# The end of the last batch: more of the heads by x^T x, and another order behind it

## The chip, the cores and the metric

The kernel runs on one core of a Trainium2 chip. The metric is the device time of one execution in microseconds. Before the change three runs gave 791.0, 791.21 and 795.83 us, median 791.21. Besides, one execution was taken with the hardware profiler; every row of a profile below comes from it.

The engines are named as in the profile: PE is TensorE (matrix products), PEld its loading of weights, DVE is VectorE, ACT is ScalarE, POOL is GpSimd, SP is SyncE, which here only issues DMAs. "SPq" is SP's instruction queue. L303 is line 303 of the kernel before. Each engine works through its own instructions strictly in the order in which the program gives them; semaphores tie the engines together.

## What is computed

Two layers, for 8 batches of 3200 rows of 256 columns. The first is a gated attention without softmax, the second a mixing of tokens:

```python
scores = z @ z.T / S                    # z: 3200 x 64
x = u * (np.maximum(scores, 0) ** 2 @ v)  # x: 3200 x 256

wq = x @ w_q                            # 3200 x 64
wk = x @ w_k                            # 3200 x 64
W_tok = wq @ wk.T / 8
out = np.maximum(W_tok @ x, 0) @ w_out  # 3200 x 256, float32
```

The second layer has no function between its first two products, so the kernel never forms `W_tok`. It builds the small matrix `wk.T @ x` (64 x 256, called the heads) from all rows of a batch, and then `wq @ heads` (the mix). Since `wk = x @ w_k`, the heads are also `w_k.T @ (x.T @ x)`: part of the rows can be brought in by x^T x, a 256 x 256 matrix, without their keys `wk`.

## The kernel before

**Tiling.** A batch of 3200 rows is cut into seven groups, numbered from 0: six of 512 rows and a last one of 128 (`widths`, L39; `LASTG` = 6). A tile is 128 rows. For each group the scores come from PE, pass through ACT or DVE (relu) and ACT or POOL (square), partly through a DMA transpose, since the scores are symmetric, and are multiplied with v on PE into two PSUM banks for each half group (L303). When a half group is finished, `gate` copies the one bank on ACT (L319), adds the other on DVE (L320), and multiplies with u on POOL into `x_sb` (L335).

**The second layer in the loop.** SP transposes x by DMA (`turn_x`, L349), PE forms queries and keys (`projections`, L366), ACT casts them to 16 bits (L379), SP transposes the keys by DMA (`turn_keys`, L384), PE multiplies keys with x into the heads (`heads`, L393). Heads are made in two portions per batch: groups 0 to 2, then the others. PE computes them in two halves of the array's rows; DVE adds them up (L406, L409, L410) into `ha`, and because one sum lies in the wrong half of the partitions, two small DMAs carry each half to the other (`cross_heads`, L415, tile `hx`), after which DVE adds again (L420, in the last batch L423). Then come, per group, the mix on PE (`mix`, L429), a relu on ACT (`mix_out`, L444 and L446, tile `rt`), the product with `w_out` on PE (`proj`, L456), the scaling (`proj_out`, ACT L484 or DVE L479) and the store by SP (L485).

**What sets the order.** The program is written out in order at build time. A small planner (L519 to L911) holds a model clock of each engine; it emits the products with v one after another and fits the other work between them, where its model says that inputs have arrived. Transfers of SP are `move`s: each has a time from which it may go and a time at which it is due, and is sent in order of the due time. `keys_landed` (L636) starts a portion of the heads when the model has all its keys. Whatever is left over when the products with v are all emitted is drained in L899 to L912.

**The last batch.** Behind the loop nothing is left to hide the second layer of the last groups. So groups 5 and 6 of batch 7 have no keys: DVE makes a second copy `xd` of their x (L329) in a free tile of pool `pz`, and `last_gram` (L495, products L499) accumulates x^T x of both in one PSUM bank. Their queries come late, by `projections` with the tile name `qq`. To have something to do meanwhile, the mixes of groups 4 and 5 of the batch before, batch 6, are put aside (`kept`, L670) and done at the end. The tail behind L913 is written out by hand:

1. x^T x of group 5; mix of the first kept group; x^T x of group 6; mix of the second kept group;
2. x^T x copied to SBUF as `G`, one half on DVE (L936), the other on ACT (L937), the second waiting for the first; PE multiplies it with `w_k` in 32 bits (`last_heads`, L509, tile `hl`); DVE adds the other groups' heads and writes `hs` (L941);
3. projection and store of the first kept group, half on ACT, half on DVE;
4. queries of groups 5 and 6 (`qq`);
5. projection and store of the second kept group;
6. mix of group 0, then for each group the mix of the next and its own projection and store.

**Buffers that matter here.** PSUM tiles of `ps_tile` (L75) have two slots, shared by scores, queries, mixes and projections; the tail's `acc_tile` uses the four banks of the products with v. `rt` has two buffers (`prt`, L71): the relu of one group must wait until the projection of the group before the last has read its own. In the tail the stores all go through SP, in order.

Of the kernel before, what the change touches and what calls it, by code (L numbers as in the profile page):

```python
# [16 lines left out]
def kernel(  # L17
# [10 lines left out]
    nc = tc.nc  # L28

    B, S, D = u.shape  # L30
# [12 lines left out]
    assert sum(widths) == S and dqk == 64 and dh == 64 and ND == 2  # L43

    FAR = 2

    GSCALE = 4.0
    C1 = GSCALE * GSCALE
# [29 lines left out]
    def acc_tile(half, r, name, dtype=FP32):  # L78
        n = W if dtype == FP32 else 2 * W
        return pacc.tile([P, n], dtype, tag=f"acc{half}{r}", name=name)  # L80
# [232 lines left out]
    def gate(b, gi, half):  # L313
        if (b, gi) not in xs:
            assert len(xs) < NX, (b, gi, list(xs))
            xs[b, gi] = px.tile([P, 2, NC, 2, dh], FP16, tag="x_sb", name="x_sb")
        n = min(2, widths[gi] // P - 2 * half)
        both = psum.tile([P, 2 * D], FP32, tag="both", name="both")
        nc.scalar.copy(out=both[:, 0 : n * D], in_=accs[half, 0][:, 0 : n * D])  # L319
        nc.vector.tensor_add(  # L320
            out=both[:, 0 : n * D], in0=accs[half, 1][:, 0 : n * D], in1=both[:, 0 : n * D]
        )
        if b == B - 1 and gi >= LASTG - 1:
            if gi < LASTG and half == 0:
                spare = pz.tile([P, NT, 2, dqk], FP16, tag="zd", name="xd")
                spare = spare[:].rearrange("p n a k -> p (n a k)")
                xds[LASTG - 1] = spare[:, 0 : 4 * D].rearrange("p (n d) -> p n d", d=D)
                xds[LASTG] = spare[:, 4 * D : 5 * D].rearrange("p (n d) -> p n d", d=D)
            nc.vector.tensor_mul(  # L329
                out=xds[gi][:, 2 * half : 2 * half + n, :].rearrange("p n d -> p (n d)"),  # L330
                in0=both[:, 0 : n * D],
                in1=us[b, gi][:, 2 * half : 2 * half + n, :].rearrange("p n d -> p (n d)"),
            )
        for r in [half] if widths[gi] == W else range(2):
            nc.gpsimd.tensor_mul(  # L335
                out=xs[b, gi][:, 0:n, :, r, :].rearrange("p n c d -> p (n c) d"),
                in0=both[:, 0 : n * D].rearrange("p (m d) -> p m d", d=dh),
                in1=us[b, gi][:, 2 * half : 2 * half + n, :].rearrange(
                    "p n (c d) -> p (n c) d", d=dh
                ),  # L340
            )
        if 2 * half + n == widths[gi] // P:
            us.pop((b, gi))
# [37 lines left out]
    def turn_keys(b, gi):  # L381
        nn = widths[gi] // P
        ks[b, gi] = pk.tile([P, 4, 2, dh], FP16, tag="kx", name="kx")
        nc.sync.dma_start_transpose(  # L384
            out=ks[b, gi][:, 0:nn, :, :].rearrange("p n a h -> p n (a h)"),
            in_=qks[b, gi][:].rearrange("p r s -> p (r s)")[:, 0 : nn * P],
        )
# [60 lines left out]
    def proj(b, gi, banks):  # L448
        rt = rts.pop((b, gi))
        nj = widths[gi] // P  # L450
        for r in halves(gi):
            n = min(2, nj - 2 * r)
            flat = rt[:, r, :, :].rearrange("p d s -> p (d s)")
            for dc in range(ND):
                for j in range(n):
                    nc.tensor.matmul(  # L456
                        out=banks[r][:, ds(j * D, D)],
                        lhsT=flat[:, ds((dc * n + j) * P, P)],
                        rhs=wo[:, dc, :],
                        start=(dc == 0 and j == 0),  # L460
                        stop=(dc == ND - 1 and j == n - 1),
                    )

    def proj_out(b, gi, banks, ways, stores=None):
        n0 = starts[gi] // P
        if stores is None:
            fo = pg.tile([P, 2, W], FP32, tag="g", name="fo")
        else:
            fo = pg.tile([P, 2, W], FP32, tag="fo", name="fo", bufs=2)
        flat_out = fo[:].rearrange("p a w -> p (a w)")  # L470
        at = 0
        for on_dve, queue, n in ways:
            sl = slice(at * D, (at + n) * D)
            if isinstance(banks, list):
                part = banks[at // 2][:, 0 : n * D]
            else:
                part = banks[:].rearrange("p a w -> p (a w)")[:, sl]
            if on_dve:
                nc.vector.tensor_scalar(  # L479
                    out=flat_out[:, sl], in0=part, scalar1=FINAL_SCALE, scalar2=None,  # L480
                    op0=AOP.mult,
                )
            else:
                nc.scalar.mul(out=flat_out[:, sl], in_=part, mul=FINAL_SCALE)  # L484
            store = lambda queue=queue, at=at, n=n, sl=sl: queue.dma_start(  # L485
                out=rows(out, b)[:, n0 + at : n0 + at + n, :],
                in_=flat_out[:, sl].rearrange("p (n d) -> p n d", d=D),
            )
            if stores is None:
                store()  # L490
            else:
                stores.append(store)
            at += n

    def last_gram(b, gi, ps):  # L495
        nj = widths[gi] // P
        for n in range(nj):
            for cc in range(ND):
                nc.tensor.matmul(  # L499
                    out=ps[:, ds(cc * D, D)],  # L500
                    lhsT=xds[gi][:, n, ds(cc * P, P)],
                    rhs=xds[gi][:, n, :],
                    start=(gi < LASTG and n == 0 and cc == 0),
                    stop=(gi == LASTG and n == nj - 1 and cc == ND - 1),
                )

# [33 lines left out]
    def at_time(t, fn):  # L540
        later.append((t, fn))

    def move(ready, due, issue, takes, fn, landed=None, may=None):
        moves.append((ready, due, issue, takes, fn, landed, may))
# [74 lines left out]
    def use_keys(b, gi):  # L619
        open_slot()  # L620
        ps = ps_tile("qk")
        projections(b, gi, ps)
        clock[PE] += 0.44 if gi < LASTG else 0.24
        ready = clock[PE] + FROM_PE
        projections_out(b, gi, ps)
        done = give(ACT, ready, 0.56)
        n = widths[gi] / P
        move(
            done + SLACK, done + 10.0, 1.28, 0.21 * n, lambda: turn_keys(b, gi),
            lambda t: at_time(t, lambda: keys_landed(b, gi)), lambda: len(ks) < NK,  # L630
        )
        close_slot(done)

    FIRST_HEADS = range(3)

    def keys_landed(b, gi):  # L636
        keyed.append((b, gi))
        for gis in FIRST_HEADS, range(3, NG if b < last else LASTG - 1):
            if gi in gis and all((b, i) in keyed for i in gis):
                add_extra(clock[PE] + 0.5, "heads", lambda gis=gis: use_heads(b, gis))  # L640

# [273 lines left out]
    def mixed(b, gi, i=None):  # L915
        if i is None:
            ps = ps_tile("mx")
            banks = [ps[:, 0, :], ps[:, 1, :]]
        else:
            ps = banks = [acc_tile(h, i % 2, "mx")[:] for h in range(len(halves(gi)))]  # L920
        mix(b, gi, banks)
        mix_out(b, gi, ps)

    def projected(b, gi, ways):
        ps = ps_tile("fo")
        proj(b, gi, [ps[:, 0, :], ps[:, 1, :]])
        proj_out(b, gi, ps, ways)

    both_ways = [(False, nc.sync, 2), (True, nc.sync, 2)]
    psg = acc_tile(1, 0, "xtx")  # L930
    last_gram(last, LASTG - 1, psg)
    mixed(*kept[0])
    last_gram(last, LASTG, psg)
    mixed(*kept[1])
    g32 = pg.tile([P, ND * D], FP32, tag="g", name="G")
    nc.vector.tensor_copy(out=g32[:, 0:D], in_=psg[:, 0:D])  # L936
    nc.scalar.copy(out=g32[:, D : 2 * D], in_=psg[:, D : 2 * D])  # L937
    psl = acc_tile(1, 1, "hl")
    last_heads(last, g32, psl[:, 0:D])
    hss[last] = psml.tile([P, D], FP16, tag="hs", name="hs")  # L940
    nc.vector.tensor_add(out=hss[last][:], in0=psl[:, 0:D], in1=hacc[last][:, 1, :])  # L941
    banks = [acc_tile(0, r, "fo") for r in range(2)]
    proj(*kept[0], banks)
    proj_out(*kept[0], banks, both_ways)
    for gi in (LASTG - 1, LASTG):
        ps = ps_tile("qq")
        projections(last, gi, ps)
        projections_out(last, gi, ps)
    projected(*kept[1], both_ways)
    for gi in range(NG):  # L950
        if gi == 0:
            mixed(last, 0, 0)
        if gi < LASTG:
            mixed(last, gi + 1, gi + 1)
        nj = widths[gi] // P
        projected(last, gi, [(True, nc.sync, nj)] if gi != LASTG - 1 else both_ways)


# [28 lines left out]
```

## Time and profile before

| what | value |
|---|---|
| median of 3 runs | 791.21 us (791.0 to 795.83) |
| profiled execution | 790.96 us, its span 789.2 us |
| PE, products | busy 763.2 us (97%) |
| PE, loading of weights | 645.7 us (82%) |
| DVE / ACT / POOL | 479.4 (61%) / 551.8 (70%) / 612.9 us (78%) |
| last product with v | begins at about 760.7 us |
| PE's longest idle time after that | 5.15 us, before 769.48 |
| stores in the tail | 12, issued between 773.07 and 786.18 us |

The span runs from the first to the last instruction of the profiled execution; the time of an execution is slightly longer. For nearly the whole span PE has work without a pause; the change concerns the last 5% or so. There the shares of busy time over the whole span say nothing; what counts is the timeline of each engine in that stretch, and, for each idle time, what ended it. A row of a timeline gives start, duration, engine, line, operation, output and inputs, and in square brackets the idle time of that engine before the row and its releaser. Rows of the same kind in a series are merged, and x8 at the end is their number.

### The profile page before, as it was taken

To read this page: it belongs to the slowest core of one execution; us is meant where nothing else is said; L and a number is where in the kernel's file an instruction comes from. 1 tells how busy PE (TensorE), PEld (TensorE's weight loads), DVE (VectorE), ACT (ScalarE), POOL (GpSimd) and SP (SyncE) were. 2 spreads that over 40 slices of the span, in tenths; PEclk is the share of its full clock that TensorE was granted. 3 is DMA by queue.
4 is the path that set the end of the run, shared out by engine and by line. 5 is a ranking of instruction groups with operands and counts; after the bars stand their busy time and mean duration, and the time that the engine had idled before them with its cause. 6 is when DMAs were issued, how large, how long until landed. Compare 5 with 4: busy or idle time off the path is not lost.

```text
span 789.2 us, 28159 instructions
## 1 busy us (share of the span) xinstructions
PE 763.2 (97%) x12373; PEld 645.7 (82%) x12373; DVE 479.4 (61%) x479; ACT 551.8 (70%) x659; POOL 612.9 (78%) x418
## 2 busy tenths in 40 slices
PE   6989999999999999999999999999999999999976
PEld 5879898887888888888788887988788888888864
DVE  5755577664685656754587635666468654675634
ACT  5766478766776677786687678866778767777624
POOL 7887799886998769877798876888789775787830
PEclk9999999999999999999999999999999999999998
DMA  7999999999999979999999999999999998899425
GB/s 192 146 172 165 177 160 179 156 225 194 204 184 189 220 164 194 152 189 216 210 162 170 187 214 199 177 151 208 193 207 165 178 225 160 183 163 194 122 56 220
DMA packets 310636, 142.57 MB, mean 181 GB/s; under 512 B 287985, under 2 KB 291953, under 8 KB 310513
## 3 DMA queue, kind: packets, MB, share of 16 engines
q1 hardware_dynamic: 303600, 124.60, 83.4%
q0 software_dynamic: 6768, 15.98, 14.8%
q8 instruction: 96, 1.57, 0.9%
q14 instruction: 28, 0.22, 0.1%
q10 hardware_dynamic: 144, 0.20, 0.1%
HBM read 59.64 MB, written 26.21 MB: 109 GB/s over the span
## 4 chain that ended last, share of the span: by engine, by line
PE 91%; DVE 3%; DMA 2%; issue 1%; ACT 1%; POOL 1%; SPq 0%; DVEq 0%; POOLq 0%; ACTq 0%
PE acc L303 66%; PE sc L224 12%; PE fo L456 6%; PE qk L366 3%; DVE g L247 2%; PE hd L393 1%; PE mx L429 1%; DVE both L320 1%; DMA v_sb<-in_v_dram 1%; DMA hx<-ha 1%; ACT both L319 1%; POOL x_sb L335 1%; DVE ha L410 0%; DMA z<-in_z_dram 0%; SPq L349 0%
## 5 line engine op out<-in xcount | busy, mean ns | idle before, releaser
L262 POOL TENSOR_TENSOR at<-g 128x1024 f16<-128x1024 f32 (+2 forms) x245 | 451.5, 1858 | 82.5 <-DVE g L247 66.5
L303 PE MATMUL acc<-v_sb,at 64*128 64x256 f16 x7312 | 499.1, 270 | 5.0 <-DVE both L320 2.5
L247 DVE TENSOR_SCALAR g<-sc 128x1024 f32<-128x1024 f32 (+2 forms) x309 | 363.9, 1197 | 153.0 <-PE sc L224 137.6
L303 PEld LDWEIGHTS <-at 64*128 64x128 f16 x7312 | 393.0, 94 | 66.8 <-issue 12.7
L260 ACT ACTIVATE at<-g 128x1024 f16<-128x1024 f32 x223 | 229.4, 1036 | 30.7 <-DVE g L247 27.2
L243 ACT ACTIVATE g<-sc 128x1024 f32<-128x1024 f32 (+1 forms) x159 | 159.2, 1003 | 60.5 <-PE sc L224 59.8
L335 POOL TENSOR_TENSOR x_sb<-both,u_sb 128x512 f16<-128x512 f32 (+1 forms) x112 | 134.4, 1207 | 64.4 <-DVE both L320 63.8
L224 PE MATMUL sc<-zT 64*128 64x512 f16 x920 | 180.2, 378 | 3.5 <-DVE g L247 3.1
L303 PE MATMUL acc<-v_sb,tt 64*128 64x256 f16 x2304 | 158.7, 269 | 0.0
L320 DVE TENSOR_TENSOR both<-acc,both 128x512 f32<-128x512 f32 (+1 forms) x104 | 69.1, 670 | 128.9 <-ACT both L319 128.4
L303 PEld LDWEIGHTS <-tt 64*128 64x128 f16 x2304 | 123.3, 94 | 11.6 <-issue 0.4
L319 ACT COPY both<-acc 128x512 f32<-128x512 f32 (+1 forms) x104 | 58.4, 566 | 65.5 <-PE acc L303 63.5
L224 PEld LDWEIGHTS <-zT 64*128 64x128 f16 x920 | 56.8, 94 | 17.6 <-issue 12.4
L484 ACT ACTIVATE fo<-fo 128x1024 f32<-128x1024 f32 (+2 forms) x50 | 44.9, 908 | 23.5 <-PE fo L456 22.1
L446 ACT ACTIVATE rt<-mx 128x1024 f16<-128x1024 f32 (+1 forms) x49 | 45.1, 931 | 22.1 <-PE mx L429 21.8
L456 PE MATMUL fo<-wo,rt 128*128 128x256 f16 x400 | 53.1, 276 | 1.2 <-ACT rt L444 0.6
L456 PEld LDWEIGHTS <-rt 128*128 128x128 f16 x400 | 35.4, 98 | 15.6 <-issue 9.6
L379 ACT CAST qk<-qk 128x512 f16<-128x512 f32 (+1 forms) x54 | 29.4, 544 | 21.6 <-PE qk L366 21.6
L366 PE MATMUL qk<-xT_sb,wqk 64*128 64x256 f16 (+1 forms) x404 | 32.2, 265 | 0.1
L366 PEld LDWEIGHTS <-wqk 64*128 64x128 f16 x416 | 22.8, 94 | 2.5 <-issue 0.5
L303 PE MATMUL acc<-v_sb,ttl 64*128 64x256 f16 x384 | 24.6, 269 | 0.0
L303 PEld LDWEIGHTS <-ttl 64*128 64x128 f16 x384 | 19.7, 94 | 3.5 <-issue 0.8
(42 smaller groups left out, 163.9 us busy)
## 6 DMA issues: line engine op xcount, KB each, us to landing
u_sb<-in_u_dram SPq DMA_DIRECT2D x48, 512.0 KB, 5.1
out_dram<-fo SPq DMA_DIRECT2D x45, 512.0 KB, 4.7
v_sb<-in_v_dram POOLq DMA_DIRECT2D x35, 320.0 KB, 6.0
zn<-in_z_dram POOLq DMA_DIRECT2D x7, 400.0 KB, 5.7
tt<-at SPq DMA_TRANSPOSE x144, 4.4
out_dram<-fo SPq DMA_DIRECT2D x6, 256.0 KB, 2.1
u_sb<-in_u_dram SPq DMA_DIRECT2D x8, 128.0 KB, 3.9
hx<-ha SPq DMA_DIRECT2D x16, 64.0 KB, 4.7
```

The costliest lines, as they stand in the source:

```text
L224: nc.tensor.matmul(out=sc[:, h, 0:gw], lhsT=zT[b][top(h), ts(ti, P)], rhs=zT[b][top(h), ds(gs, gw)], start=True, stop=True,)
L243: nc.scalar.activation(out=g[:, hs, 0:w], in_=sc[:, hs, 0:w], func=RELU, scale=GSCALE)
L247: nc.vector.tensor_scalar(out=g[:, hs, 0:w], in0=sc[:, hs, 0:w], scalar1=0.0, scalar2=GSCALE, op0=AOP.max, op1=AOP.mult,)
L260: nc.scalar.square(out=out, in_=g[:, hs, 0:w])
L262: nc.gpsimd.tensor_mul(out=out, in0=g[:, hs, 0:w], in1=g[:, hs, 0:w])
L303: nc.tensor.matmul(out=accs[half, r][:, ds((j % 2) * D, D)], lhsT=weights(b, gi, ti, j)[top(r), :], rhs=vs[b][top(r), ti, :], start=(first ...
L319: nc.scalar.copy(out=both[:, 0 : n * D], in_=accs[half, 0][:, 0 : n * D])
L320: nc.vector.tensor_add(out=both[:, 0 : n * D], in0=accs[half, 1][:, 0 : n * D], in1=both[:, 0 : n * D])
L335: nc.gpsimd.tensor_mul(out=xs[b, gi][:, 0:n, :, r, :].rearrange("p n c d -> p (n c) d"), in0=both[:, 0 : n * D].rearrange("p (m d) -> p m ...
L366: nc.tensor.matmul(out=ps[:, r, 0 : n * P], lhsT=wqk[top(r), c, :, :].rearrange("p t h -> p (t h)"), rhs=xTs[b, gi][top(r), 0:n, c, :], st ...
L446: nc.scalar.activation(out=out, in_=ps[:, 0:nr, 0 : ND * n * P], func=RELU)
L456: nc.tensor.matmul(out=banks[r][:, ds(j * D, D)], lhsT=flat[:, ds((dc * n + j) * P, P)], rhs=wo[:, dc, :], start=(dc == 0 and j == 0), sto ...
```

## The change

- A new name `GRAM` = `LASTG` - 2 = 4. In the last batch groups 4, 5 and 6 have no keys: their `xd` is made on DVE, and `last_gram` accumulates all three. Before these were groups 5 and 6. The transposed keys of group 4 are no longer made, while its queries still come from the loop, as before.
- The second portion of heads of the last batch is then group 3 alone (before 3 and 4). In the emitted program the order of PE moves these heads, now 8 products, from behind the last product with v to a place 134 products earlier; the DMAs of the crossing, `hx`, move in SP's queue from behind the x transposes of groups 5 and 6 to ahead of both; and the sums of `ha` move on DVE ahead of group 5's gate.
- The tail has another order. Both kept mixes come first, then x^T x of the three groups without a break. The first kept group's projection and its outputs stand ahead of `last_heads`. The mixes of groups 0 and 1 stand ahead of the second kept group's projection; on ACT all four halves of their relu come before that group's output. Group 6's output is on ACT, where it was on DVE.

The number of instructions of PE stays the same (24741 with weights and branches): 8 products of the heads with their loads go, 8 of x^T x come. DVE has two products more and one output less.

```diff
+    GRAM = LASTG - 2
...
-        if b == B - 1 and gi >= LASTG - 1:
-            if gi < LASTG and half == 0:
+        if b == B - 1 and gi >= GRAM:
+            if gi == GRAM and half == 0:
                 spare = pz.tile([P, NT, 2, dqk], FP16, tag="zd", name="xd")
                 spare = spare[:].rearrange("p n a k -> p (n a k)")
-                xds[LASTG - 1] = spare[:, 0 : 4 * D].rearrange("p (n d) -> p n d", d=D)
-                xds[LASTG] = spare[:, 4 * D : 5 * D].rearrange("p (n d) -> p n d", d=D)
+                for i in range(GRAM, NG):
+                    cols = ds((i - GRAM) * 4 * D, widths[i] // P * D)
+                    xds[i] = spare[:, cols].rearrange("p (n d) -> p n d", d=D)
...
-                    start=(gi < LASTG and n == 0 and cc == 0),
+                    start=(gi == GRAM and n == 0 and cc == 0),
...
-        move(
-            done + SLACK, done + 10.0, 1.28, 0.21 * n, lambda: turn_keys(b, gi),
-            lambda t: at_time(t, lambda: keys_landed(b, gi)), lambda: len(ks) < NK,
-        )
+        if b < last or gi < GRAM:
+            move(
+                done + SLACK, done + 10.0, 1.28, 0.21 * n, lambda: turn_keys(b, gi),
+                lambda t: at_time(t, lambda: keys_landed(b, gi)), lambda: len(ks) < NK,
+            )
...
-        for gis in FIRST_HEADS, range(3, NG if b < last else LASTG - 1):
+        for gis in FIRST_HEADS, range(3, NG if b < last else GRAM):
...
     both_ways = [(False, nc.sync, 2), (True, nc.sync, 2)]
+    mixed(*kept[0])
+    mixed(*kept[1])
     psg = acc_tile(1, 0, "xtx")
-    last_gram(last, LASTG - 1, psg)
-    mixed(*kept[0])
-    last_gram(last, LASTG, psg)
-    mixed(*kept[1])
+    for gi in range(GRAM, NG):
+        last_gram(last, gi, psg)
     g32 = pg.tile([P, ND * D], FP32, tag="g", name="G")
     nc.vector.tensor_copy(out=g32[:, 0:D], in_=psg[:, 0:D])
     nc.scalar.copy(out=g32[:, D : 2 * D], in_=psg[:, D : 2 * D])
+    banks = [acc_tile(0, r, "fo") for r in range(2)]
+    proj(*kept[0], banks)
+    proj_out(*kept[0], banks, both_ways)
     psl = acc_tile(1, 1, "hl")
     last_heads(last, g32, psl[:, 0:D])
     hss[last] = psml.tile([P, D], FP16, tag="hs", name="hs")
     nc.vector.tensor_add(out=hss[last][:], in0=psl[:, 0:D], in1=hacc[last][:, 1, :])
-    banks = [acc_tile(0, r, "fo") for r in range(2)]
-    proj(*kept[0], banks)
-    proj_out(*kept[0], banks, both_ways)
     for gi in (LASTG - 1, LASTG):
         ps = ps_tile("qq")
         projections(last, gi, ps)
         projections_out(last, gi, ps)
+    mixed(last, 0, 0)
+    mixed(last, 1, 1)
     projected(*kept[1], both_ways)
     for gi in range(NG):
-        if gi == 0:
-            mixed(last, 0, 0)
-        if gi < LASTG:
+        if 0 < gi < LASTG:
             mixed(last, gi + 1, gi + 1)
-        nj = widths[gi] // P
-        projected(last, gi, [(True, nc.sync, nj)] if gi != LASTG - 1 else both_ways)
+        ways = [(gi != LASTG, nc.sync, widths[gi] // P)]
+        projected(last, gi, ways if gi != LASTG - 1 else both_ways)
```

## The prediction

> **What bounds the kernel now.** I read the page first, then the chain of waits, then the end of the run engine by engine in the timeline, because every edit touches only the last batch's end.
>
> ```profile
> span 789.2 us, 28159 instructions
> ```
>
> The profiled execution took 790.96 us, so 1.76 us lie outside its span; the median of the runs shown is 791.21, 0.25 above it. TensorE (PE) works without a pause into the tail, which its timeline shows (start, duration, work, idle time before it and its releaser):
>
> ```profile
> 760.94 0.41 PE L393 MATMUL hd<-x_sb,kx 64*64 64x256 f16 x8
> 761.97 0.41 PE L393 MATMUL hd<-x_sb,kx 64*64 64x256 f16 x8 [0.61 <-DMA kx<-qk]
> 762.31 1.05 PE L499 MATMUL xtx<-xd 128*128 128x256 f16 x8
> 763.29 0.39 PE L429 MATMUL mx<-qk,hs 64*128 64x256 f16 x4
> 763.62 0.39 PE L499 MATMUL xtx<-xd 128*128 128x256 f16 x2
> 763.94 0.39 PE L429 MATMUL mx<-qk,hs 64*128 64x256 f16 x4
> 769.48 2.07 PE L509 MATMUL hl<-G,wk 128*128 128x256 f32 x4 [5.15 <-DVE G L936]
> 771.35 1.59 PE L456 MATMUL fo<-wo,rt 128*128 128x256 f16 x8
> 772.87 0.83 PE L366 MATMUL qq<-xT_sb,wqk 64*128 64x256 f16 x12
> 774.16 1.03 PE L456 MATMUL fo<-wo,rt 128*128 128x256 f16 x8 [0.46 <-ACT qk L379]
> 775.13 0.61 PE L429 MATMUL mx<-qk,hs 64*128 64x256 f16 x8
> 776.37 1.10 PE L456 MATMUL fo<-wo,rt 128*128 128x256 f16 x8 [0.63 <-ACT rt L444]
> ```
>
> PE stands idle for 5.15 us before L509, waiting for the copy G of x^T x. VectorE (DVE) and the queue of SyncE (SP) say why:
>
> ```profile
> 759.59 1.19 SPq L384 DMA_TRANSPOSE kx<-qk  x1
> 761.12 4.75 SPq L349 DMA_TRANSPOSE xT_sb<-x_sb  x2
> 765.96 1.18 SPq L415 DMA_DIRECT2D hx<-ha  x2
> ```
>
> ```profile
> 768.66 0.43 DVE L423 TENSOR_TENSOR ha<-ha,hx 128x256 f32<-128x256 f32 x1 [4.73 <-DMA hx<-ha]
> 769.01 0.42 DVE L936 COPY G<-xtx 128x256 f32<-128x256 f32 x1
> 771.59 0.42 DVE L941 TENSOR_TENSOR hs<-hl,ha 128x256 f16<-128x256 f32 x1 [2.17 <-PE hl L509]
> ```
>
> x^T x itself is done about 764. But G stands behind L423 on DVE, L423 waits for the crossing hx, and hx is issued at 765.96, behind two transposes of x. The restart is slow besides:
>
> ```profile
> 770.00:771.00 1.00, 1.00 (x4) 0.75 (x3) 0.00 (x0) 0.00 (x0) 0.00 (x0) 0.50 0.00 0
> 776.00:777.00 1.00, 0.63 (x6) 0.44 (x7) 0.55 (x1) 1.00 (x3) 0.00 (x0) 1.00 0.30 119
> 780.00:787.00 7.00, 4.26 (x37) 2.63 (x36) 4.73 (x6) 3.43 (x7) 0.00 (x0) 0.94 0.99 401
> ```
>
> In these stretches the third number from the end is the granted clock, the next the DMA share: 0.50 after the idle time, 1.00 again at 776. From 780 on the stores fill the DMA engines (0.99, 401 GB/s), so the end follows the rhythm of the stores, not the last instruction.
>
> **The loop's edits, costed at nothing.** Group 4's key transpose (1.19 us of SP at 759.59) goes, and with it the 0.61 us wait of the heads. The remaining 8 heads products, now of group 3 alone, stand 134 products earlier in PE's order, and hx two transposes earlier in SP's.
>
> ```profile
> 748.95 6.97 PE acc L303 x125
> ```
>
> At 6.97/125 = 0.056 us a product that place is about 760.94 - 134 x 0.056 = 753.4. Its keys:
>
> ```profile
> 746.39 1.19 SPq L384 DMA_TRANSPOSE kx<-qk  x1
> ```
>
> ```profile
> kx<-qk SPq DMA_TRANSPOSE x1, 3.9
> ```
>
> They land at 746.39 + 3.9 = 750.3, which leaves 3.1 us. Behind the heads queue all remaining products, so each microsecond beyond that would cost one. From 753.8 DVE's two sums of ha (L409, L410) take some 1.4 us (at most 0.69 each, as the xd product of that width below); from the start of hx's issue to L423 it was 768.66 - 765.96 = 2.7. So hx is there by 758, and L423, which stands behind the last group's xd and so behind 761, doesn't wait. The second half of the heads leaves the end; the first half moves up by its 0.41 us at most, so PE's later work slips by 0.3.
>
> Group 4 gets two xd products on DVE beside GpSimd's (POOL's) x_sb:
>
> ```profile
> 757.31 0.69 DVE L329 TENSOR_TENSOR xd<-both,u_sb 128x512 f16<-128x512 f32 x1
> 757.36 1.78 POOL L335 TENSOR_TENSOR x_sb<-both,u_sb 128x512 f16<-128x512 f32 x1 [5.15 <-DVE both L320]
> ```
>
> ```profile
> 742.82 1.28 POOL L335 TENSOR_TENSOR x_sb<-both,u_sb 128x512 f16<-128x512 f32 x1
> ```
>
> ```profile
> 748.46 3.75 POOL L262 TENSOR_TENSOR at<-g 128x1024 f16<-128x1024 f32 x2
> ```
>
> That is 2 x 0.69 = 1.4 us of DVE and 2 x (1.78 - 1.28) = 1.0 of POOL at 742 to 749. The last squares then end some 0.5 later than 748.46 + 3.75 = 752.2; PE's order takes them at about 753.6 and 754.7, so two microseconds cover it. Without that cover it costs up to 1.4; nothing in it can gain. I take 0.
>
> **The tail, step by step.** The remaining rows of ScalarE (ACT) and the transposes:
>
> ```profile
> 769.46 0.37 ACT L937 COPY G<-xtx 128x256 f32<-128x256 f32 x1 [3.80 <-DVE G L936]
> 772.44 0.60 ACT L484 ACTIVATE fo<-fo 128x512 f32<-128x512 f32 x1 [2.61 <-PE fo L456]
> 773.52 0.75 ACT L379 CAST qk<-qq 128x512 f16<-128x512 f32 x2 [0.48 <-PE qq L366]
> ...
> 775.73 3.25 ACT L444 ACTIVATE rt<-mx 128x512 f16<-128x512 f32 x6
> ```
>
> ```profile
> 763.68 2.19 SPq L349 DMA_TRANSPOSE xT_sb<-x_sb  x1
> ```
>
> ```profile
> xT_sb<-x_sb SPq DMA_TRANSPOSE x1, 5.5
> ...
> xT_sb<-x_sb SPq DMA_TRANSPOSE x1, 3.3
> ```
>
> ```profile
> DMA to landing us min/median/max: 2.9/5.9/9.6
> ```
>
> ```profile
> 777.51 6.44 DVE L479 TENSOR_SCALAR fo<-fo 128x1024 f32<-128x1024 f32 x5 [0.96 <-PE fo L456]
> ```
>
> 1. The loop's products end by 760.94 + 0.3 = 761.25. Two kept mixes, by the 0.61 for 8: 761.85. x^T x has 18 products instead of 10; 8 take 763.29 - 762.31 = 0.98, so 18 take 2.2: 764.05. The 8 added cost 1.0.
> 2. The first kept projection, now ahead of hl, takes 1.05 (as the 8 x^T x products of that shape): 765.1. Beside it run G on DVE (0.24 behind PE, as hs behind hl: 771.59 - 771.35; then 0.42) and on ACT (0.37), to 765.1: just hidden.
> 3. hl took 771.35 - 769.48 = 1.87 at clock 0.50; PE has not rested, so I halve it: 766.05. hs follows 0.24 + 0.42 later: 766.7. Bounds: 1.87 if the clock stayed low, 0.94.
> 4. What is late next: the transposes of x, which nobody waited for before. They follow POOL, not the change: issued 0.3 later than at 761.12 and 763.68, landing after 5.5 and 3.3, at 766.9 and 767.3. PE stands in order before the first mix with both projections (0.83 for 12). The long one ends 767.35, the short one, held by the second landing, 767.5. The mix of groups 0 and 1 starts at **767.55** instead of 775.13: 7.6 earlier.
> 5. The new order gives some back. The kept second projection now comes behind these mixes. It needs the slot of the long projection, free after ACT's cast at 768.15, and runs to 769.2. ACT, free of both casts at 768.3, does two halves of rt at 3.25/6 = 0.54 each, to 769.4. The next two write the buffer that the kept projection reads (prt has two), so 769.4 to 770.5; then the kept output, 0.60, to 771.1. Group 0's projection starts at 769.2, group 1's needs the kept output's slot: 771.15. Its output starts 777.51 - 776.37 = 1.14 later on DVE: 772.3. Before, the five 1288 ns outputs ran back to back, the second from 777.51 + 1.29 = 778.8. So 6.5 of the 7.6 remain.
> 6. From there both kernels do the same: one output per 1.3 us, the DMA engines full. Group 6's output on ACT instead of DVE ends earlier, but its store stands behind full DMA engines: 0. Bounds 0 to 0.4 gained.
>
> Sum: 790.96 - 6.5 = 784.5, or 784.7 on the median's footing. Of it about 5.2 is the idle time, 1.5 the half clock on L509 and L456 (0.94 and 0.54), 1.1 the two short waits at 774.16 and 776.37; against it 1.0 for x^T x and the new waits.
>
> The clock decides 1.5 of this. The Trainium skill, TensorE: Matmul & The Clock Gate, "A second HAM failure mode: psum-queue depth-cycling", says that frequent short pauses between groups of matmuls can make the clock fall again, which speaks against an end with pauses of 0.6 to 0.9 us. The trace disagrees here: at 776 PE was busy 0.63 of the time at a clock of 1.00.
>
> **The rivals.**
> - Transposes sooner: with the shortest landing, 2.9, the second is there at 766.9, ACT's casts end 0.8 earlier, and group 1's projection starts at about 770.4: 784.0. For it: the DMA engines are nearly empty there. Against: 5.5 and 3.3 in this very place. By the Trainium skill, DMA: Bandwidth & Descriptors, "Anatomy of one DMA", a transfer costs 2.0 us and its bytes at 436 GB/s, an estimate of 2.3 for these 128 KB; then hs would be last and the time 783.4. The 3.3 measured is longer.
> - Transposes later: the median 5.9 for the second gives 769.9, 2.6 later: 787.3. For it: the median; against: it is one of a loop whose DMA engines are full.
> - Slower than before: the same wait at its far end. PE's mixes stand behind the short projection, which before had until 772.87. Each microsecond of landing costs one; 6.5 are used up from a landing of 9.8 after issue. The longest in the whole trace is 9.6. At 12 it would be 787.3 + 6.1 = 793.4.
> - The clock falls in the short pauses: 1.5 is not won, 786.2. Against: the row at 776.
> - The loop stalls on DVE, POOL or the moved heads, or the crossing isn't sooner because of it: up to 1.4 lost, 786.1. Against: the two to three microseconds of cover.
>
> **How the numbers follow.** Forecast 0.60, sooner 0.15, later 0.12, clock 0.05, loop 0.06, slower 0.02. The range, 783.0 to 787.5, takes in all but the far ends of sooner and later and the slower case. About 1% is what a measurement of this kernel can tell from no change, 7.9 us here: below 783.3 lies the far end of "sooner" and a little of the forecast, 0.10; above 799.1 almost nothing, 0.02; within 1% 0.88.
>
> **What would show it.** In the changed profile: no idle time of PE before hl, a granted clock of 1.00 there and hl at about 0.95 us; hx issued before 757 and L423 without a wait; the short projection waiting on xT_sb; one wait of about 0.8 before group 1's projection, released by ACT; DMA share near 1 to the end. I am wrong if the transposes land much earlier or later than 767, if PE pauses between 743 and 757, or if the outputs lose their 1.3 us rhythm.

## The result, and the profile after

The changed kernel takes **786.62 us** (median of 6 runs, 785.18 to 788.46) against 793.12 for the kernel before (6 runs, 791.0 to 795.83): a ratio of 0.9923, 95% interval 0.9907 to 0.9939, so 5 to 7 us less, 0.8%, inside the range of 783.0 to 787.5. The profiled execution took 785.18 us, and its page begins:

```profile
span 783.4 us, 28161 instructions
```

This kernel's executions differ by several us in their front part, which the change doesn't touch (the first heads of the last batch start between 738.85 and 744.66 in the traces of this study). To compare traces to a fraction of a microsecond, I therefore measure a **tail** in each: from the first heads of the last batch to the end of the span. In PE's timeline they are one row of 24 products, of before and then of after:

```profile
741.08 0.85 PE L393 MATMUL hd<-x_sb,kx 64*64 64x256 f16 x24
```

```profile
740.92 0.85 PE L395 MATMUL hd<-x_sb,kx 64*64 64x256 f16 x24
```

The tail was 789.2 - 741.08 = 48.1 us and is 783.4 - 740.92 = 42.5: 5.6 less. Lines behind the edited places have moved by a few. PE's timeline of after:

```profile
743.90 0.39 PE L225 MATMUL sc<-zT 64*128 64x512 f16 x2 [0.50 <-DVE ha L408]
749.34 0.59 PE L225 MATMUL sc<-zT 64*128 64x512 f16 x4
754.44 0.41 PE L395 MATMUL hd<-x_sb,kx 64*64 64x256 f16 x8
762.11 0.60 PE L431 MATMUL mx<-qk,hs 64*128 64x256 f16 x8
762.64 2.14 PE L501 MATMUL xtx<-xd 128*128 128x256 f16 x18
764.62 1.04 PE L458 MATMUL fo<-wo,rt 128*128 128x256 f16 x8
765.49 1.03 PE L511 MATMUL hl<-G,wk 128*128 128x256 f32 x4
766.45 0.61 PE L368 MATMUL qq<-xT_sb,wqk 64*128 64x256 f16 x8
767.50 0.28 PE L368 MATMUL qq<-xT_sb,wqk 64*128 64x128 f16 x2 [0.43 <-DMA xT_sb<-x_sb]
767.57 0.28 PE L431 MATMUL mx<-qk,hs 64*128 64x256 f16 x1
768.26 1.92 PE L458 MATMUL fo<-wo,rt 128*128 128x256 f16 x16
771.75 1.03 PE L458 MATMUL fo<-wo,rt 128*128 128x256 f16 x8 [1.25 <-DVE fo L481]
```

The idle time of 5.15 us before hl is gone. hl takes 766.45 - 765.49 = 0.96 instead of 1.87, and the only waits left from there to group 1's projection at 771.75 are 0.43 for the second transpose and 1.25 for the kept output. New is a wait in the loop: 0.50 at 743.90, released by a copy on DVE. The queue of SP and DVE show why hl is free:

```profile
756.09 1.11 SPq L417 DMA_DIRECT2D hx<-ha  x2
762.38 3.94 SPq L351 DMA_TRANSPOSE xT_sb<-x_sb  x2
```

```profile
742.43 0.82 DVE L331 TENSOR_TENSOR xd<-both,u_sb 128x512 f16<-128x512 f32 x1
743.18 0.68 DVE L408 COPY ha<-hd 128x512 f32<-128x512 f32 x1
747.13 1.02 DVE L331 TENSOR_TENSOR xd<-both,u_sb 128x512 f16<-128x512 f32 x1
763.56 0.95 DVE L425 TENSOR_TENSOR ha<-ha,hx 128x256 f32<-128x256 f32 x1
764.82 0.42 DVE L939 COPY G<-xtx 128x256 f32<-128x256 f32 x1 [0.31 <-PE xtx L501]
766.56 0.42 DVE L947 TENSOR_TENSOR hs<-hl,ha 128x256 f16<-128x256 f32 x1 [0.17 <-PE hl L511]
771.01 6.95 DVE L481 TENSOR_SCALAR fo<-fo 128x512 f32<-128x512 f32 x6 [4.03 <-ACT fo L486]
```

The crossing hx is issued at 756.09 instead of 765.96, its sum L425 waits for nothing, and G waits only for x^T x. In the table by stretches, the granted clock (third number from the end) is 1.00 where before it had 0.50, and the stores still fill the DMA engines:

```profile
766.00:767.00 1.00, 1.00 (x11) 0.42 (x9) 0.81 (x2) 0.15 (x1) 0.00 (x0) 1.00 0.58 131
774.00:781.00 7.00, 4.27 (x37) 2.63 (x36) 4.42 (x5) 3.73 (x8) 0.00 (x0) 1.00 1.00 407
```

### The profile page after: what moved, and what is told of

It is laid out like the page before. It is cut to its first block, busy times and chain, and to the rows that moved or that the text cites. A ratio compares the mean times of both kernels' runs of the same rounds, so it can differ in the third digit from the quotient of the medians.

```text
span 783.4 us, 28161 instructions
## 1 busy us (share of the span) xinstructions
PE 762.4 (97%) x12373; PEld 644.5 (82%) x12373; DVE 479.1 (61%) x480; ACT 552.1 (70%) x660; POOL 613.9 (78%) x418
## 4 chain that ended last, share of the span: by engine, by line
PE 89%; DVE 4%; DMA 3%; issue 1%; ACT 1%; POOL 1%; POOLq 0%; DVEq 0%; ACTq 0%
PE acc L304 66%; PE sc L225 12%; PE fo L458 6%; PE qk L368 2%; PE mx L431 1%; PE hd L395 1%; DVE g L248 1%; DVE both L321 1%; DMA kx<-qk 1%; ACT both L320 1%; DMA v_sb<-in_v_dram 1%; POOL x_sb L337 1%; POOL at L263 0%; DVE ha L412 0%; DMA z<-in_z_dram 0%
```

## The experiments

Each kernel ran beside the kernel before on the same chip. Ratios are to that, with a 95% interval. Where there is one execution only, its time says little, since the front part differs by several us; such effects are read from the tails. Up to the stores a tail repeats well: five executions whose order on PE is the same up to there (after, e4, e6, e7 and e9b) reach the kept mixes 21.18 to 21.19 us behind the first heads. For the stretch of the stores behind it there is no such repeat, so 0.2 or 0.3 at the end of a span is not certain.

**e1_gram_only: x^T x of group 4, with the old order of the end.** The changed kernel, with its last part as before:

```
-    mixed(*kept[0])
-    mixed(*kept[1])
     psg = acc_tile(1, 0, "xtx")
-    for gi in range(GRAM, NG):
-        last_gram(last, gi, psg)
+    last_gram(last, GRAM, psg)
+    last_gram(last, LASTG - 1, psg)
+    mixed(*kept[0])
+    last_gram(last, LASTG, psg)
+    mixed(*kept[1])
     ...   (G, hl, kept projection, both projections, mixes, outputs as before)
```

> Group 4's heads by x^T x and so the earlier heads and crossing, but the tail in the order of before (x^T x of group 4 simply ahead of that of group 5). Theory: the crossing hx behind the x transposes is what held G, so this part alone brings nearly all. PE then rests only about 1 us before hl (the two copies of G one after the other), hl stays near 1 us, the second output of the last series on DVE starts about 0.4 us later than the 773.0 us of the changed kernel, and the time is 5 to 6 us below before. Rival, the new order of the tail is what hides G: less than 3 us below before.

786.71 us, ratio 0.9926 (0.9902 to 0.995); tail 785.0 - 741.25 = 43.75, 4.4 less than before. The heads by x^T x carry most of the gain; the order adds 43.75 - 42.48 = 1.27. PE's timeline shows what the order removes, two rests at hl, where G's halves have nothing to hide behind:

```profile
765.62 0.70 PE L511 MATMUL hl<-G,wk 128*128 128x256 f32 x2 [0.19 <-DVE G L940]
767.08 0.70 PE L511 MATMUL hl<-G,wk 128*128 128x256 f32 x2 [0.76 <-ACT G L941]
```

**e2_order_only: the new order, with x^T x of the last two groups only.**

```
-    GRAM = LASTG - 2
+    GRAM = LASTG - 1
```

> The new order of the tail, with group 4's heads by its keys as before. Theory: G still waits for hx, which still stands behind the x transposes; PE rests about 4 us before hl (the first kept projection now fills part), hl runs at half clock again in about 2 us, and the gain over before is 0.5 to 2 us. Rival: if the order hides G by itself, 4 us or more below before.

791.81 us, ratio 0.9985 (0.9966 to 1.0004); tail 791.9 - 743.79 = 48.1, no gain at all in this execution. The idle time before hl did shrink, but the half clock behind it lasted longer:

```profile
772.14 2.08 PE L511 MATMUL hl<-G,wk 128*128 128x256 f32 x4 [3.79 <-DVE G L939]
```

```profile
770.00:771.00 1.00, 0.00 (x0) 0.00 (x0) 0.00 (x0) 0.00 (x0) 0.00 (x0) 0.91 0.38 96
777.00:778.00 1.00, 1.00 (x8) 0.78 (x7) 0.00 (x0) 0.21 (x1) 0.00 (x0) 0.68 0.00 0
```

A second with a clock of 0.91 was at half for 0.18 of it, so the fall came at 770.82; by 0.68 the rise came at 777.64. That is 6.82 us, 5.50 of them with work in them. Before, the same reading gives 769.06 to 772.46: 3.40 us, 2.98 with work.

```profile
769.00:770.00 1.00, 0.52 (x1) 0.50 (x2) 0.43 (x2) 0.37 (x1) 0.00 (x0) 0.53 0.00 0
772.00:773.00 1.00, 1.00 (x10) 0.64 (x10) 0.04 (x2) 0.56 (x1) 0.00 (x0) 0.77 0.00 0
```

The longer stretch alone can cost (5.50 - 2.98) / 2 = 1.26, as much as the order had won in e1.

**e11_order_again and e12_order_third: e2 two more times**, unchanged, to see whether an execution's phase decides this.

> The program of e2_order_only once more, for another execution of it. Theory: in e2 the order gained its 1.3 us as in e1, and an execution's phase took it back: the granted clock changes only on a grid of 3.41 us (in e2 it was 0.50 from 770.82 to 777.64, two steps; before, from 769.06 to 772.46, one step). Then this execution shows a half-clock stretch at the idle time before hl of 3.41 or 6.83 us and nothing between; with 3.41 the stretch from the first heads to the end of the span is 46.6 to 47.1, with 6.83 it is 47.5 to 48.2. Rival: the new order gains nothing without x^T x of group 4: 48.1 with either length.

> The same program a third time, with the same expectations: theory, 46.6 to 47.1 where the half-clock stretch lasts 3.41 us and 47.5 to 48.2 where it lasts 6.83; rival, 48.1 with either.

794.82 and 792.73 us, one execution each; the kernel before, once beside them, took 789.95. PE's timeline and the clock of e11, then of e12:

```profile
773.14 2.08 PE L511 MATMUL hl<-G,wk 128*128 128x256 f32 x4 [3.92 <-DVE G L939]
```

```profile
772.00:773.00 1.00, 0.00 (x0) 0.00 (x0) 0.68 (x2) 0.00 (x0) 0.00 (x0) 0.53 0.00 0
778.00:779.00 1.00, 1.00 (x7) 0.74 (x6) 0.00 (x0) 0.21 (x1) 0.00 (x0) 0.55 0.00 0
```

```profile
771.42 2.08 PE L511 MATMUL hl<-G,wk 128*128 128x256 f32 x4 [4.08 <-DVE G L939]
```

```profile
769.00:770.00 1.00, 0.00 (x0) 0.00 (x0) 0.00 (x0) 0.00 (x0) 0.00 (x0) 0.79 0.44 113
776.00:777.00 1.00, 1.00 (x9) 0.81 (x8) 0.00 (x0) 0.50 (x2) 0.00 (x0) 0.80 0.00 0
```

Both stretches are again two steps long, 772.06 to 778.90 and 769.58 to 776.40, so the case with one step, which would have told the two theories apart directly, didn't come up. The tails are 793.1 - 744.66 = 48.4, above the theory's bound of 48.2, and 791.0 - 742.79 = 48.2. What does tell is the time from hl to the end against the half clock with work in it: 19.58 us at 4.98 (e12), 19.76 at 5.50 (e2), 19.96 at 5.76 (e11). That is 0.38 us for 0.78, half a microsecond for each, as a half clock should cost. By that slope the new order would take 18.6 at the 2.98 of before, which itself needed 789.2 - 769.48 = 19.7. By this estimate the order gains about 1 us also without group 4's x^T x, and the longer half clock took it back in these executions. No run shows it: the three tails, 48.1 to 48.4, are also what the rival said.

**e3_xd_alone: the kernel before, with group 4's xd products on DVE and nobody who reads them.**

```
-        if b == B - 1 and gi >= LASTG - 1:
-            if gi < LASTG and half == 0:
+        if b == B - 1 and gi >= LASTG - 2:
+            if gi == LASTG - 2 and half == 0:
```

> The kernel before with nothing changed but two more xd products on DVE for group 4, whose result nobody reads. Theory: on DVE the first xd stands ahead of the copy of the first heads out of PSUM, whose slot the next scores need; PE waits about 0.5 us there and about 0.3 us at the scores some 6 us later, and all behind it comes 0.8 us later, so 0.5 to 1 us slower than before. Rival, PE lost the time in the changed kernel to the moved heads: no wait there, the loop ends within 0.2 us of before, no change of the time.

793.26 us, ratio 0.9994 (0.9969 to 1.0019); tail 790.9 - 741.85 = 49.05, 0.93 more. The medians can't tell this from no change. Its half clock lasted two steps too (767.94 to 774.76), so the end of the loop is the cleaner place. PE's timeline of e3, beside the row at 761.97 of before:

```profile
744.83 0.39 PE L224 MATMUL sc<-zT 64*128 64x512 f16 x2 [0.50 <-DVE ha L407]
763.71 0.41 PE L394 MATMUL hd<-x_sb,kx 64*64 64x256 f16 x8 [0.61 <-DMA kx<-qk]
```

The loop's last heads start 763.71 - 741.85 = 21.86 behind the first, before 761.97 - 741.08 = 20.89: the two xd products cost the loop 0.97 us, and the 0.50 of after's timeline is here too, released by the same copy of the first heads.

**e4_crossing_late: the changed kernel, with the crossing hx back behind the transposes of x.**

```
-        move(done + SLACK, done + 2.0, 0.55, 0.1, lambda: cross_heads(b, 0))
+        when = done + SLACK if b < last else 1e6
+        move(when, done + 2.0, 0.55, 0.1, lambda: cross_heads(b, 0))
```

> The changed kernel, but the two crossing DMAs hx are issued by SP behind the x transposes of groups 5 and 6 again. Theory: hx is issued at about 766.4 us, G waits on DVE until about 769, PE rests some 4 us, hl falls to half clock (1.9 us), and 4 to 5.5 us of the gain are lost: 788 to 790 us in a profiled execution whose changed kernel takes 785. Rival, the crossing wasn't what held the end but the heads' late keys: less than 1.5 us lost.

791.81 us, ratio 0.9988 (0.9972 to 1.0005); tail 787.7 - 739.82 = 47.9. Of the 5.64 us won, 0.24 is left. The half clock lasted one step, as before (768.68 to 772.10, 3.42 us), so these two tails can be compared. The queue of SP, DVE and PE show the old chain again:

```profile
765.12 1.18 SPq L417 DMA_DIRECT2D hx<-ha  x2
```

```profile
767.84 0.43 DVE L425 TENSOR_TENSOR ha<-ha,hx 128x256 f32<-128x256 f32 x1 [5.30 <-DMA hx<-ha]
```

```profile
768.65 2.08 PE L511 MATMUL hl<-G,wk 128*128 128x256 f32 x4 [4.10 <-DVE G L940]
```

So nearly all of the gain hangs on the place of the two crossing DMAs in SP's queue. That x^T x serves to let them go early is read from the program: without it they wait for group 4's heads, whose keys PE got only at 761.97.

**e5_xd_behind: the changed kernel, with group 4's xd products later on DVE**, behind the copy of the first heads.

```
-            nc.vector.tensor_mul(
+            double = lambda x=xds[gi], ug=us[b, gi]: nc.vector.tensor_mul(
     ...
+            if gi == GRAM:
+                at_time(clock[PE] + (2.8 if half == 0 else 1.7), double)
+            else:
+                double()
```

> The changed kernel with one edit: the two xd products of group 4 stand later on DVE, the first behind the copy of the first heads and the relu after it, the second behind one more relu. PE's order is the same. Theory: the copy frees its PSUM slot in time, the wait of 0.50 us before the scores goes, and the loop's products end about 0.8 us sooner after the first heads (20.4 instead of 21.2 us); counted from the start of the first heads (24 products) to the end of the span, 42.5 becomes 41.7. Rival, POOL's slower x_sb beside xd is what costs: the wait stays or moves, less than 0.3 us gained.

One execution, 786.75 us; tail 785.0 - 743.48 = 41.5, 0.96 less. PE's wait at the scores is gone, and the kept mixes start 20.21 behind the first heads instead of 762.11 - 740.92 = 21.19:

```profile
745.79 0.38 PE L225 MATMUL sc<-zT 64*128 64x512 f16 x2
750.91 0.59 PE L225 MATMUL sc<-zT 64*128 64x512 f16 x4
763.69 0.60 PE L435 MATMUL mx<-qk,hs 64*128 64x256 f16 x8
```

Behind the first heads, the scores of the first row come 0.67 us sooner than in after (2.31 for 2.98) and those of the second 0.99 (7.43 for 8.42). With e3 this is the cost from both sides: 0.97 added alone, 0.96 to 0.98 taken away.

**e6_kept_on_dve: the second kept output wholly on DVE**, instead of half on ACT and half on DVE.

```
-    projected(*kept[1], both_ways)
+    projected(*kept[1], [(True, nc.sync, 4)])
```

> The changed kernel with the whole output of the second kept group on DVE (1.3 us) instead of half on ACT behind four relus and then half on DVE. Theory: the 1.25 us wait of PE before group 1's projection is this output, held up by ACT's relus and by DVE's half standing behind ACT's; it falls to 0.2 us or less, and the second output of the last series starts 1 us sooner: 42.5 us from the first heads to the end become 41.5. Rival: the last stretch is bound by the stores, and 1 us less of waiting moves the end by less than 0.3.

One execution, 787.33 us; tail 785.6 - 743.39 = 42.2, only 0.27 less, though group 1's projection starts 29.70 behind the first heads instead of 771.75 - 740.92 = 30.83, with no wait:

```profile
773.09 1.03 PE L458 MATMUL fo<-wo,rt 128*128 128x256 f16 x8
```

Of 1.13 us won there, 0.86 is given back behind it. The stretches at the end of e6, then of after, suggest where:

```profile
782.00:783.00 1.00, 0.00 (x0) 0.00 (x0) 0.00 (x0) 0.00 (x0) 0.00 (x0) 0.50 1.03 391
783.00:783.20 0.20, 0.00 (x0) 0.00 (x0) 0.00 (x0) 0.00 (x0) 0.00 (x0) 0.50 0.93 323
783.50:784.00 0.50, 0.00 (x0) 0.00 (x0) 0.00 (x0) 0.00 (x0) 0.00 (x0) 0.50 0.06 20
```

```profile
781.50:782.00 0.50, 0.00 (x0) 0.00 (x0) 0.00 (x0) 0.00 (x0) 0.00 (x0) 0.50 0.60 207
```

In after the DMA engines stop together, about 0.6 of the way through that half microsecond. In e6 they are full nearly to 783.2, and then a share of 0.06 goes on to 784.0, as much as one engine of sixteen, alone, for some 0.8 us. From the last data to the end of the span both need 1.6 us (783.4 - 781.8 and 785.6 - 784.0). Fifteen engines thus end 783.2 - 743.39 = 39.8 behind the first heads, in after 781.8 - 740.92 = 40.9: the lag of the one accounts for what was given back. No run takes the lag away alone.

**e7_short_query_later: the short query projection behind the mix of group 0**, so that its transpose is waited for later.

```
     for gi in (LASTG - 1, LASTG):
         ...
+        if gi < LASTG:
+            mixed(last, 0, 0)
-    mixed(last, 0, 0)
```

> The changed kernel with the short projection (queries of group 6) behind the mix of group 0 instead of ahead of it. Theory: the landing of the second x transpose is what the first mix waits for, so the mix starts right behind hs, 0.4 to 0.6 us sooner, and the end comes 0.3 us sooner. Rival: what stands behind waits for ACT's cast anyway: the mix is sooner, the end is not (less than 0.1).

One execution, 782.88 us; tail 781.1 - 738.85 = 42.25, 0.23 less. PE's timeline of e7 has the first mix 26.12 behind the first heads instead of 26.65, 0.53 sooner:

```profile
764.97 0.39 PE L431 MATMUL mx<-qk,hs 64*128 64x256 f16 x4
```

Less than half of that is seen behind it: group 1's projection starts 769.44 - 738.85 = 30.59 behind the first heads instead of 30.83, as it waits for the kept output and not for the mix.

**e8_all_three: e5, e6 and e7 together.**

> The three edits together: xd later on DVE, the kept output on DVE, the short projection behind the first mix. Theory, if the three waits stand one behind the other: 0.8 + 1.0 + 0.3, so about 40.4 us from the first heads to the end of the span against 42.5 for the changed kernel and 48.1 for the kernel before, and a time of 1.0% below before. Rival: the transposes of x, which follow POOL, or the stores take the place of what is removed: more than 41.3 us.

784.47 us, ratio 0.9886 (0.9866 to 0.9906); tail 784.8 - 743.80 = 41.0, 1.48 less. That is about 0.96 + 0.27 + 0.23, and lies between the theory's 40.4 and the rival's 41.3. The end has one DMA engine behind the others again: fifteen are done at 782.4, the last at 783.2.

**e9b_store_left_out: e6 without the store of the second kept output.** Its rows of the output aren't written, so 512 KB less go out.

```
-    projected(*kept[1], [(True, nc.sync, 4)])
+    ps = ps_tile("fo")
+    proj(*kept[1], [ps[:, 0, :], ps[:, 1, :]])
+    proj_out(*kept[1], ps, [(True, nc.sync, 4)], [])
```

> The changed kernel with the whole second kept output on DVE (as in the run with that one edit, 42.2 us from the first heads to the end of the span), and the store of that output, 512 KB, left out: these rows of the result are not written. Theory: from the first output of the last series on, the end is set by the stores, which keep the DMA engines full at some 400 GB/s; 512 KB less are 1.0 to 1.3 us less, so about 41.1 us. Rival, the end follows PE and DVE: less than 0.3 us gained.

One execution, 786.85 us; tail 785.1 - 743.02 = 42.1, 0.13 less than e6. The theory falls: the volume of that store isn't what limits the end of e6, and the engines are full behind it all the same.

```profile
776.00:782.00 6.00, 3.23 (x28) 1.89 (x25) 3.46 (x4) 2.91 (x7) 0.00 (x0) 0.97 1.00 404
```

DVE alone hands out six outputs of 512 KB in 7.48 us here, which is some 420 GB/s. So a DMA share of 1.00 doesn't show that the stores set the pace; which of the two does stays open.

**e10b_kept_first: e8 with the second kept projection ahead of all mixes.**

```
         if gi < LASTG:
+            projected(*kept[1], [(True, nc.sync, 4)])
             mixed(last, 0, 0)
     mixed(last, 1, 1)
-    projected(*kept[1], [(True, nc.sync, 4)])
```

> The kernel with all three edits, and the second kept group's projection moved ahead of the mix of group 0, so that its 512 KB are stored about 1 us sooner, while the DMA engines are still idle, and its buffer rt is read before ACT needs it. Theory: if the stores set the end, about 0.5 to 0.9 us less than the 41.0 us from the first heads to the end of the span, 40.1 to 40.5, and a time 1.1 to 1.4% below before. Rival: PE's later mixes cost as much as the earlier store brings: 41.0 or more.

784.54 us, ratio 0.9899 (0.9866 to 0.9932); tail 782.6 - 742.15 = 40.5, 2.03 less than after and the shortest of all, at the upper end of the theory's range. The first output goes out sooner, the DMA engines are no longer full throughout (0.89), and no single engine ends late:

```profile
772.00:780.00 8.00, 5.43 (x48) 3.33 (x44) 5.57 (x5) 4.74 (x10) 0.00 (x0) 1.00 0.89 362
```

But all engines are done only at about 781.0, 38.9 behind the first heads, where fifteen of e8's were done 782.4 - 743.80 = 38.6 behind. What e10b has over e8 is thus the missing lag, and that the earlier store brings anything isn't shown.

e8 and e10b have lower medians than the changed kernel, and by the tails both are faster than it. Of the timed intervals, e8's ends at 0.9906, just below the changed kernel's, which begins at 0.9907; e10b's overlaps with both. Why one DMA engine falls behind in e6, e8 and e9b and not in after or e10b stays open: it is not the volume of the kept store, and no run here tells more.

## Why the prediction was right, step by step

The forecast was 784.7 us with a tail 6.5 shorter; measured were 786.62 and a tail 5.64 shorter. The chain of causes held: e4 shows that the early crossing carries it, e1 that the order adds 1.27 of it. The forecast counted from 791.21 for the kernel before, which over six runs took 793.12. That the medians differ by 6.5, just as forecast, is luck, since the tails differ by 5.64.

- **The loop's edits, costed at nothing: wrong by 0.9 us, the term that was mis-sized.** The loop ended at 762.11, not at 761.25, and e3 and e5 put 0.97 and 0.96 on the two xd products. I had looked for their cost at POOL's squares, where I saw two microseconds of cover. It arose on DVE at once: xd at 742.43 stands ahead of the copy of the first heads at 743.18, that copy frees the PSUM slot of the next scores, and PE waited 0.50 for it at 743.90. Against e5, 0.67 is lost by these scores and 0.3 more by those at 749.34, behind the second xd. The heads that moved cost about what was forecast: 0.35 by e5, whose products with v are done 20.21 behind the first heads (before, 760.94 - 741.08 = 19.86), for 0.3.
- **Steps 1 and 2 held.** x^T x took 764.62 - 762.64 = 1.98 for 18 products (2.2 forecast), and the kept projection hid both copies of G.
- **Step 3 held.** hl took 0.96 (0.94 forecast); the clock stayed at 1.00, since PE didn't rest. The rival in which short pauses lower the clock fell: with the 0.43 and the 1.25 of after's timeline the clock was 1.00.
- **Step 4 came out right by two errors that cancel.** The first mix started at 767.57, forecast 767.55. But the second transpose was issued at 765.12, over 1 us later than I had it, as the loop and POOL were late, and landed after 2.33 instead of 3.3. The chain of waits of after shows both:

```profile
765.12 2.33 DMA xT_sb<-x_sb
```

  The wait was where I had put it, and the rival of sooner transposes came true in its landing only. "They follow POOL, not the change" was wrong: in all nine traces without group 4's key transpose ahead of them the two transposes landed after 3.5 to 3.9 and 2.3 us, in all five with it (before, e2, e3, e11, e12) after 5.4 to 5.6 and 3.3 to 3.6. So the change itself brought the sooner landing, and only that the two errors were of one size was luck. Nor were the DMA engines nearly empty there before: from 762 to 763 their share was 1.00. The Trainium skill, DMA: Bandwidth & Descriptors, "Anatomy of one DMA", gives the figures behind the prediction's 2.3 for DMAs that GpSimd issues. These are issued by SyncE, so the 2.33 doesn't confirm it.
- **Step 5 was short by 0.6.** Group 1's projection started at 771.75, not 771.15. I had the kept output's ACT half end the wait; but DVE's half of the same tile waits for ACT's (the row at 771.01, released by ACT's fo), so 0.6 more stands in the path. ACT's four halves of rt ahead of it were as forecast. In ACT's timeline:

```profile
768.20 2.28 ACT L446 ACTIVATE rt<-mx 128x512 f16<-128x512 f32 x4
770.37 0.60 ACT L486 ACTIVATE fo<-fo 128x512 f32<-128x512 f32 x1
```

- **Step 6 held in its numbers.** From there one output follows another by 1.3 us, with a DMA share of 1.00. That the end follows the rhythm of the stores isn't shown, as e9b says. The loop's 0.9 was nearly all paid back by the landing, so that the 0.6 of step 5 makes up most of the 6.5 - 5.64 = 0.86 that the forecast was too large.

## What to carry to other kernels

Before an extra product goes on an engine "with room", look at what stands behind it in that engine's order, and whether that frees a PSUM slot for TensorE: here two products of together 1.8 us (0.82 and 1.02) on an engine with idle time cost 0.96 at the end. A DMA that one late step waits for belongs ahead of the transposes that nobody waits for yet. A transfer that a change takes away can make its neighbours land sooner, here by 1 us and more. And where two engines share the copy of one PSUM tile, count them one behind the other until the trace shows them side by side.

## What the runs showed of the hardware

- **The granted clock changes on a grid.** The half-clock stretches at the idle time lasted 3.40 us before, 3.42 in e4, and 6.82 to 6.84 in e2, e3, e11 and e12: one or two steps of 3.4, wherever the idle time ended. In the trace of before the clock next falls at 786.12 (its mean is 0.56 from 786 to 787), 13.66 or four steps behind the rise at 772.46. A step that held 1.08 us of rest (772.06 to 773.14 in e11) was followed by another at half; one that held 0.42 (769.06 to 769.48 before) was not. The Trainium skill, TensorE: Matmul & The Clock Gate, "What's actually happening", gives a free-running window of 3413 ns; the lengths here agree. So what an idle time costs behind its end depends on where the grid lies in that execution: half of 2.98 us before, half of 5.76 in e11.
- **DVE and POOL slow each other where they overlap, and it is the later one that pays.** POOL's timeline of after:

```profile
742.66 1.72 POOL L337 TENSOR_TENSOR x_sb<-both,u_sb 128x512 f16<-128x512 f32 x1
763.26 1.83 POOL L337 TENSOR_TENSOR x_sb<-both,u_sb 128x256 f16<-128x256 f32 x2 [0.91 <-DVE both L321]
```

  The first took 1.28 before, where no xd stood beside it. In turn the xd products of group 4 took 0.82 and 1.02 us, against 0.69 for one of that width before, and the sum L425, beside the second of these rows, 0.95 against 0.43. The loss is each time the overlap less 0.15 us, as if the later instruction waited for the earlier: the first xd began 0.28 before POOL's square ended at 742.71 and lost 0.13, the second 0.48 before 747.61 and lost 0.33, and the x_sb of the first row 0.59 before the end of xd and lost 0.44.
- **The transposes of x landed later where another transpose was issued shortly ahead of them.** With group 4's key transpose 1.5 us ahead in SP's queue (759.59 and 761.12 before), the two transposes of x landed 1.5 us or more and 1.0 us or more later, in five traces against nine. Why isn't shown.
